# Fillers, paired rstd and moved GpSimd work in the first stage of a spectral and GEGLU layer

## Chip, cores and metric

The kernel runs on one core of a Trainium2 chip. The metric is device time in microseconds (us), the median of several runs. The core has five queues that are spoken of here: PE (TensorE, products; its weight loads are listed as PEld), DVE (VectorE), ACT (ScalarE), POOL (GpSimd) and SP (SyncE, which issues most transfers).

## The reference, cut to what matters

Two sublayers, each with a residual and a layer norm in front, on x of 2048 rows and 576 columns in bf16. The first multiplies the two-dimensional real Fourier transform by a complex weight. The second is a GEGLU feed-forward layer.

```
def _layernorm(x, axis=-1, eps=1e-5):
    m = jnp.mean(x, axis=axis, keepdims=True)
    v = jnp.var(x, axis=axis, keepdims=True)
    return (x - m) / jnp.sqrt(v + eps)
...
X = rfft2(layernorm(x));  y = irfft2(X * (w_r + 1j * w_i))
h = x + y
h2 = h + (gelu(n @ w_gate) * (n @ w_up)) @ w_down      # n = layernorm(h)
```

## The kernel before, in words

The order on every queue is the order of the program text: the author writes it out by hand, and each engine works through its own instructions in that order, waiting on semaphores that the framework derives from the data.

**First stage** (lines 73 to 450, the one that is changed). x is held as 16 tiles h of 128 rows by 576 columns (`h_sb[:, h, :]`), loaded in six chunks (L72: tiles 0-1, 2-3, 4-5, 6-7, 8-11, 12-15). Each tile goes through these steps:

- Statistics into `mv`: on DVE by `ln_dve` (L115 to 119, called through `sd`) for tiles 0, 2, 4, 6, 8, 10 and 12 to 15; on ACT by `ln_act` (L121) for 1, 3, 5, 7, 9 and 11, which `ln_fin` on POOL turns into a variance (L128, L129).
- `ln_rstd` on POOL (L133, L134): adds eps and takes the power -0.5 for a range of tiles.
- `norms(lo, hi)` (L337): per tile a normalisation on DVE into `xn` (L137), then `row16(h)` on PE.
- `row16` (L288): first `fill`, which is a number of filler products of the identity with a slice of x into the PSUM tile that the real products overwrite afterwards; then four products of 256 columns with the table F16 (L298), a Fourier transform over 16 rows; then `row16_rest` (L311), two small products for the remaining columns, which for tiles 12 to 15 come later.
- Evictions from PSUM into `Bt` on ACT (`evict`, L322, for two tiles; `evict4`, L328, for the remaining columns of four tiles, the last of these on DVE).

PSUM tiles come from one pool of four, given out in turn (`two`). A filler that writes such a tile waits until its previous user has been evicted.

Between these steps the text places the making of tables. POOL makes index tables by iota, the column angles `kd` (L198, three operations of 290 columns, and L199, a rounding over all 870 columns), clears `DF`, `DI` and the ends of `Zts`, and gathers reversed rows of both weights into `wm` (L364, indirect transfers). DVE makes the row angles (`angle_a`, `angle_b`, `angle_c`, for k in `first` or `rest`) and `phases` and `drop_sign` for the column angles. ACT makes their sines (`sine`, `cosine`, `col_sin`). SP then moves `wm_r` into `WR` (L412), transposes `TF` into `TI` (L262) and copies parts of the column table `DT` into `DF`, `DI` and `DS` (L424).

The stage ends with the products into `pt` (L435), their scaled copies `G16` on ACT (L443), and three fillers into the second half of the same PSUM tile.

**Behind it:** f2 (L479) multiplies Bt by the column tables, f3 (L494, L495) combines halves, DVE multiplies by the weights (`wmul`), i3 and `inv_cols` (L570 to L619) go back, and `add_rows` (L742) adds the result to x. Then comes the feed-forward part: gate and up products (L877) and down products (L897), in four chunks of 512 rows.

Of the kernel before, what the change touches and what calls it, by code (L numbers as in the profile page):

```python
# [10 lines left out]
ALU = mybir.AluOpType  # L11
# [12 lines left out]
D = 576  # L24
# [17 lines left out]
def kernel_body(  # L42
# [14 lines left out]
    G = nc.gpsimd  # L57
    T = nc.tensor
# [7 lines left out]
    def two(name):  # L66
        return psum.tile([P, 2, 512], FP32, name=name, tag="two", bufs=4)

    h_sb = keep.tile([P, H, D], BF16, name="h_sb")
# [28 lines left out]
    ident = keep.tile([P, P], BF16, name="ident")  # L98
# [7 lines left out]
    DF = keep.tile([P, 2, 2, JH], BF16, name="DF")  # L106
    DI = keep.tile([P, 2, 2, JH], BF16, name="DI")
    DS = keep.tile([P, 2, 2, JH], BF16, name="DS")
    mv = keep.tile([P, H, 2], FP32, name="mv")
    rstd = keep.tile([P, H], FP32, name="rstd")  # L110
# [4 lines left out]
    def ln_dve(dst, h):  # L115
        st = roll.tile([P, 2, 6], FP32, name="st", tag="st", bufs=3)
        V.bn_stats(st[:, 0, :], h_sb[:, h, 0:DH])  # L117
        V.bn_stats(st[:, 1, :], h_sb[:, h, DH:D])  # L118
        V.bn_aggr(dst[:, h, :], st[:])  # L119

    def ln_act(h):  # L121
        for i, fn, sc in ((0, ACT.Identity, 1.0 / D), (1, ACT.Square, 1.0 / D**0.5)):
            junk = roll.tile([P, D], BF16, name="junk", tag="junk", bufs=2)
            A.activation(junk[:], h_sb[:, h, :], fn, scale=sc, accum_out=mv[:, h, i : i + 1])

    def ln_fin(hs):
        sq = roll.tile([P, H], FP32, name="sq", tag="sq", bufs=2)
        G.tensor_tensor(sq[:, hs], mv[:, hs, 0], mv[:, hs, 0], ALU.mult)  # L128
        G.tensor_tensor(mv[:, hs, 1], mv[:, hs, 1], sq[:, hs], ALU.subtract)  # L129

    def ln_rstd(dst, src, lo, hi):
        sl = slice(lo, hi)
        G.tensor_scalar(dst[:, sl], src[:, sl, 1], 1e-5, None, op0=ALU.add)  # L133
        G.tensor_tensor(dst[:, sl], dst[:, sl], mhalf[:, sl], ALU.pow)  # L134
# [33 lines left out]
    def tmp(name, shape, dtype=I32):  # L168
        return scr.tile(shape, dtype, name=name)

    def iota(t, pattern, base=0, cm=0):
        G.iota(t, pattern=pattern, base=base, channel_multiplier=cm, allow_small_or_imprecise_dtypes=True)
# [18 lines left out]
    iJ = tmp("iJ", [P, JP], FP32)  # L191
    iota(iJ[:], [[1, 2], [2, JH]])
    iDs = tmp("iDs", [P, 3], FP32)
    G.tensor_scalar(iDs[:], iD[:], 1.0 / D, None, op0=ALU.mult)
    pd, kd = tmp("pd", [P, 3, JP], FP32), tmp("kd", [P, 3, JP], FP32)
    C23 = 8388608.0
    for t in range(3):
        G.tensor_scalar(kd[:, t, :], iJ[:], iDs[:, t : t + 1], C23, op0=ALU.mult, op1=ALU.add)  # L198
    G.tensor_scalar(kd[:], kd[:], -C23, -float(D), op0=ALU.add, op1=ALU.mult)  # L199
    rev = tmp("rev", [P, 1])  # L200
    iota(rev[:], [[0, 1]], 2 * P - 1, -2)

# [19 lines left out]
    def drop_sign(dst, src):  # L222
        V.tensor_scalar(
            dst.bitcast(I32),
            src.bitcast(I32),
            1,
            1,
            op0=ALU.logical_shift_left,
            op1=ALU.logical_shift_right,
        )  # L230
# [3 lines left out]
    def angle_a(sl):  # L234
        n = sl.stop - sl.start
        V.scalar_tensor_tensor(
            pr[:, sl],
            q16[:].unsqueeze(1).to_broadcast([P, n, P]),
            s2p[:, 0:1],
            ks[:, sl].unsqueeze(2).to_broadcast([P, n, P]),  # L240
            op0=ALU.mult,
            op1=ALU.add,
        )

    def angle_b(sl):
        V.tensor_scalar(pr[:, sl], pr[:, sl], 2047, None, op0=ALU.bitwise_and)
        V.tensor_scalar(ab[:, sl], pr[:, sl], -1024.0, None, op0=ALU.add)

    def angle_c(sl):
        drop_sign(ab[:, sl], ab[:, sl])  # L250

    def sine(sl):
        A.activation(TF[:, sl, 2, :], pr[:, sl], ACT.Sin, bias=pib[:], scale=-2.0 * PI / S)

    def cosine(sl):
        A.activation(TF[:, sl, 1, :], ab[:, sl], ACT.Sin, bias=nhpib[:], scale=2.0 * PI / S)
# [15 lines left out]
    def row_table():  # L272
        V.tensor_tensor(
            F16[:, 0:2, :],
            fs[:].unsqueeze(1).to_broadcast([P, 2, P]),
            mask[:].unsqueeze(1).to_broadcast([P, 2, P]),
            ALU.mult,
        )
        V.tensor_scalar(F16[:, 2, :], F16[:, 0, :], -1.0, None, op0=ALU.mult)
# [3 lines left out]
    def fill(dst, n):  # L283

        for _ in range(n):
            T.matmul(dst, lhsT=ident[:], rhs=h_sb[:, 2, 0:512], start=True, stop=True)  # L286

    def row16(h):  # L288
        if h % 2 == 0 or h == H - 1:
            ps_f[h] = two("f2t")  # L290
        if h % 4 == 0:
            ps_f["f4", h] = two("f4")
        f2t, b = (ps_f[h], 0) if h in ps_f else (ps_f[h - 1], 1)
        fill(f2t[:, b, :], 10 if h == 0 else 1 if h < 12 else 0)
        x = xn[:, h, :]
        for t in range(2):
            for n, d0 in ((0, t * P), (1, DH + t * P)):
                T.matmul(  # L298
                    f2t[:, b, t * 2 * P : (t + 1) * 2 * P],
                    lhsT=x[:, d0 : d0 + P],  # L300
                    rhs=F16[:, n : n + 2, :],
                    start=(n == 0),
                    stop=(n == 1),
                )
        if h < 12:
            row16_rest(h)

    def row16_rest(h):
        o = (h % 4) * P
        for p0, d0 in ((0, 256), (64, 512)):  # L310
            T.matmul(  # L311
                ps_f["f4", h - h % 4][p0 : p0 + 64, 0, o : o + P],
                lhsT=xn[:, h, d0 : d0 + 64],
                rhs=F16[:, 0, :],
                start=True,
                stop=True,
            )

    def evict(*hs):
        for h in hs:  # L320
            n = 1 if h >= H - 2 else 2
            A.copy(  # L322
                Bt[:, 0:4, :].rearrange("p t (c h l) -> p (t c) h l", c=16, h=16)[:, :, h : h + n, :],
                ps_f[h][:, 0:n].rearrange("p h (tc l) -> p tc h l", l=8),
            )

    def evict4(h):
        (V.tensor_copy if h == 12 else A.copy)(  # L328
            Bt[:, 4, :].rearrange("p (c h l) -> p h c l", c=16, h=16)[:, h : h + 4, :, :],
            ps_f["f4", h][:, 0].rearrange("p (h c l) -> p h c l", h=4, c=16),  # L330
        )

    def sd(*hs):
        for h in hs:
            ln_dve(mv, h)

    def norms(lo, hi):  # L337
        for h in range(lo, hi):
            normalise(V, xn[:, h, :], mv, rstd, h)
            row16(h)  # L340
# [14 lines left out]
    first, rest = slice(0, 2), slice(2, 9)  # L355
    ln_act(1)
    ln_act(3)
    sd(0)
    row_table()
    sd(2)  # L360
    ln_fin(slice(1, 4, 2))
    ln_rstd(rstd, mv, 0, 4)
    for t, w in zip(wm, (A_w_r, A_w_i)):
        G.indirect_dma_start(  # L364
            out=t[:],
# [1 line left out]
            in_=w.rearrange("(a r) j -> a (r j)", r=8),  # L367
            in_offset=bass.IndirectOffsetOnAxis(ap=rev[:, 0:1], axis=0),
        )
    sd(4)  # L370
    ln_act(5)
    ln_act(7)
    norms(0, 4)
    evict(0, 2)
    evict4(0)
    sd(6)
    ln_fin(slice(5, 8, 2))
    ln_rstd(rstd, mv, 4, 8)
    G.memset(DF[:], 0.0)
    G.memset(DI[:], 0.0)  # L380
    for z in Zts:
        G.memset(z[:, :, J:], 0.0)
    angle_a(first)
    angle_b(first)
    angle_c(first)
    sine(first)
    cosine(first)
    norms(4, 8)
    ln_act(9)
    ln_act(11)  # L390
    phases()
    drop_sign(kd[:], pd[:])
    sd(8)
# [5 lines left out]
    evict4(4)  # L399
    col_sin(1, pd, zerob)  # L400
    col_sin(0, kd, hpib)
    sd(12)
    norms(8, 12)
    sd(13)
    ln_rstd(rstd, mv, 12, 14)
    sd(14, 15)
    ln_rstd(rstd, mv, 14, 16)
    evict(8, 10)
# [21 lines left out]
    evict4(12)  # L430
    angle_b(rest)
    pt = two("pt")
    for x in range(2):
        for p0 in (0, 64):
            T.matmul(  # L435
                pt[p0 : p0 + 64, 0, x * P : (x + 1) * P],
                lhsT=F16[:, 0, 64 * x : 64 * x + 64],
                rhs=ident[:],
                start=True,
                stop=True,  # L440
            )
    for sign in range(2):
# [4 lines left out]
            scale=G_SCALE if sign == 0 else -G_SCALE,  # L447
        )
    sine(rest)
    fill(pt[:, 1, :], 3)  # L450

    def weights():
        V.tensor_scalar(WI[:, 9 : H + 1, 0:J], wm[1][:].rearrange("p (r j) -> p r j", r=8), -1.0, None, op0=ALU.mult)
# [397 lines left out]
    for h in range(4, H):  # L851
        b = 6 * (h // 2 - 2)
# [4 lines left out]
        b = h // 4 * NFT - NFT + 3 * (h % 4) + 2 + 12 * (h < 8)  # L857
# [6 lines left out]
    for tcnk in range(4):  # L864
        for gi in range(NG):
# [5 lines left out]
            for i in range(FQ):  # L871

                gu = two("gu")
                for r in range(NR):
                    for c in range(2):
# [3 lines left out]
                            lhsT=w[rows, r, i * P : (i + 1) * P],  # L879
                            rhs=hl[tcnk % 2][rows, r, :],  # L880
                            start=(r == 0),
                            stop=(r == NR - 1),
# [7 lines left out]
        for st in range(4):  # L890
            h = tcnk * 4 + st
            last = h == H - 1
            acc = two("acc")
            for c in range(2):
                cc = slice(c * DH, (c + 1) * DH)
                for f in range(NFT):
                    T.matmul(  # L897
                        acc[:, c, 0:DH],
                        lhsT=p_sb(f)[:, st * P : (st + 1) * P],
                        rhs=wd[f // NWA][:, f % NWA, cc],  # L900
                        start=(f == 0),
                        stop=(f == NFT - 1),
# [60 lines left out]
```

## Time and profile before

| What | Value |
|---|---|
| Median of three runs | 510.25 us (509.28 to 511.15) |
| The profiled execution's own time | 510.21 us |
| Its span, first to last instruction | 508.3 us |
| PE busy | 493.3 us, 97% of the span |
| DVE, ACT, POOL busy | 212.7, 151.6, 28.4 us |
| First product of f2 (L479) | 31.73 us |
| First gate product (L877) | 79.37 us |

An entry of a timeline gives start, duration, engine, line, operation, the result and its sources, and how many there were in a row; brackets hold the idle time of the engine before it and what ended it. Matmuls overlap, so their durations are longer than their spacing. The table of stretches gives busy time of PE, PEld, DVE, ACT and POOL with the number of instructions, then the clock granted to PE (1.00 is full), the share of the transfer engines and GB/s. "issue" in the chain of work is time in which the engine waited for nothing that the profile shows.

### The profile page before, as it was taken

To read this page: it belongs to the slowest core of one execution; us is meant where nothing else is said; L and a number is where in the kernel's file an instruction comes from. 1 tells how busy PE (TensorE), PEld (TensorE's weight loads), DVE (VectorE), ACT (ScalarE), POOL (GpSimd) and SP (SyncE) were. 2 spreads that over 40 slices of the span, in tenths; PEclk is the share of its full clock that TensorE was granted. 3 is DMA by queue.
4 is the path that set the end of the run, shared out by engine and by line. 5 is a ranking of instruction groups with operands and counts; after the bars stand their busy time and mean duration, and the time that the engine had idled before them with its cause. 6 is when DMAs were issued, how large, how long until landed. Compare 5 with 4: busy or idle time off the path is not lost.

```text
span 508.3 us, 9886 instructions
## 1 busy us (share of the span) xinstructions
PE 493.3 (97%) x4334; PEld 291.7 (57%) x4334; DVE 212.7 (42%) x421; ACT 151.6 (30%) x265; POOL 28.4 (6%) x75
## 2 busy tenths in 40 slices
PE   6799999999999999999999999999999999999996
PEld 2367775555558774444468744444578544444775
DVE  7879974689662015433311034433201233333001
ACT  6879984232220002323210023233200133332000
POOL 8300010111110000000000000000000000000000
PEclk9899999999999999999999999999999999999999
DMA  9408957779970009998730089987500488870000
GB/s 295 157 19 160 242 156 208 150 150 188 189 155 0 1 36 195 201 190 151 148 62 1 1 181 196 190 165 153 98 0 1 120 167 158 157 148 1 12 14 25
DMA packets 88200, 61.54 MB, mean 121 GB/s; under 512 B 22813, under 2 KB 86749, under 8 KB 88157
## 3 DMA queue, kind: packets, MB, share of 16 engines
q1 hardware_dynamic: 87869, 59.72, 59.0%
q0 software_dynamic: 288, 1.18, 0.6%
q8 instruction: 34, 0.56, 0.5%
q14 instruction: 9, 0.07, 0.1%
HBM read 52.65 MB, written 2.36 MB: 108 GB/s over the span
## 4 chain that ended last, share of the span: by engine, by line
PE 91%; DVE 3%; POOL 2%; ACT 1%; issue 1%; DMA 1%; POOLq 0%
PE gu L877 55%; PE acc L897 28%; PE pq_ps L479 2%; PE cs_ps L619 1%; PE eo_ps L572 1%; PE y_ps L742 1%; PE eo_ps L570 1%; DMA Bt<-hrow 1%; PE gh_ps L495 1%; POOL rstd L134 1%; DVE xn L137 1%; ACT Bt L322 1%; DVE h_sb L787 1%; PE f2t L298 1%; PE gh_ps L494 1%
## 5 line engine op out<-in xcount | busy, mean ns | idle before, releaser
L877 PE MATMUL gu<-Bt,wgu 64*128 64x512 bf16 x2592 | 281.5, 376 | 1.0 <-DMA Bt<-hrow 1.0
L877 PEld LDWEIGHTS <-wgu 64*128 64x128 bf16 x2592 | 131.2, 94 | 148.1 <-issue 2.0
L885 ACT ACTIVATE g_sb<-gu 128x512 f32<-128x512 f32 x144 | 86.1, 598 | 302.8 <-PE gu L877 302.8
L886 DVE TENSOR_TENSOR P_sb<-g_sb,gu 128x512 bf16<-128x512 f32 x144 | 98.8, 686 | 153.0 <-ACT g_sb L885 153.0
L897 PEld LDWEIGHTS <-P_sb 128*128 128x128 bf16 x1152 | 112.4, 98 | 30.6 <-issue 2.4
L897 PE MATMUL acc<-wd,P_sb 128*128 128x288 bf16 x768 | 99.3, 286 | 0.0
L909 DVE TENSOR_TENSOR h_sb<-h_sb,acc 128x576 bf16<-128x576 bf16 x15 | 11.3, 755 | 118.2 <-PE acc L897 118.2
L897 PE MATMUL acc<-wd_a,P_sb 128*128 128x288 bf16 x384 | 52.3, 286 | 0.5 <-DVE h_sb L905 0.5
L298 PE MATMUL f2t<-F,xn 128*128 128x256 bf16 x64 | 11.5, 320 | 3.7 <-DVE xn L137 3.7
L286 PE MATMUL f2t<-h_sb,ident 128*128 128x512 bf16 x21 | 9.6, 547 | 4.3 <-DMA h_sb<-in_A_x_dram 4.3
L479 PE MATMUL pq_ps<-DT,Bt 128*128 128x290 bf16 x64 | 12.2, 286 | 0.0
L767 DVE TENSOR_SCALAR hrow<-h_sb,mv,rstd 128x1152 bf16<-128x1152 bf16 x14 | 12.1, 867 | 0.0
L134 POOL TENSOR_TENSOR rstd<-rstd,mhalf 128x1 f32<-128x1 f32 (+2 forms) x17 | 11.4, 673 | 1.4
L298 PEld LDWEIGHTS <-xn 128*128 128x128 bf16 x64 | 6.8, 111 | 8.1 <-DVE xn L137 5.4
L619 PEld LDWEIGHTS <-EO 128*128 128x128 bf16 x96 | 9.1, 96 | 3.0 <-issue 0.2
L479 PEld LDWEIGHTS <-Bt 128*128 128x128 bf16 x96 | 9.3, 97 | 2.5
L487 ACT CAST pq<-pq_ps 128x580 bf16<-128x580 f32 x15 | 9.8, 662 | 1.7 <-PE pq_ps L479 1.6
L133 POOL TENSOR_SCALAR rstd<-mv 128x1 f32<-128x1 f32 (+2 forms) x17 | 4.0, 235 | 112.6 <-DVE mv L119 112.4
L322 ACT CAST Bt<-f2t 128x1024 bf16<-128x1024 f32 (+1 forms) x9 | 8.1, 926 | 6.9 <-PE f2t L298 6.9
L117 DVE BATCH_NORM_STATS2 st<-h_sb 128x6 f32<-128x288 bf16 x22 | 9.8, 444 | 0.0
L118 DVE BATCH_NORM_STATS2 st<-h_sb 128x6 f32<-128x288 bf16 x22 | 9.7, 442 | 0.0
L619 PE MATMUL cs_ps<-DI,EO 128*128 128x290 bf16 x32 | 9.1, 285 | 0.0
(130 smaller groups left out, 252.3 us busy)
## 6 DMA issues: line engine op xcount, KB each, us to landing
wgu<-in_B_w_gate_dram SPq DMA_DIRECT2D x48, 432.0 KB, 5.1
wgu<-in_B_w_up_dram SPq DMA_DIRECT2D x48, 432.0 KB, 6.5
wd<-in_B_w_down_dram SPq DMA_DIRECT2D x2, 1728.0 KB, 7.5
wd_a<-in_B_w_down_dram SPq DMA_DIRECT2D x1, 1728.0 KB, 14.6
out_dram<-h_sb SPq DMA_DIRECT2D x3, 576.0 KB, 3.5
h_sb<-in_A_x_dram SPq DMA_DIRECT2D x4, 288.0 KB, 3.3
h_sb<-in_A_x_dram SPq DMA_DIRECT2D x2, 576.0 KB, 5.2
WR<-in_A_w_r_dram SPq DMA_DIRECT2D x1, 650.2 KB
```

The source lines that it names most:

```text
L117: V.bn_stats(st[:, 0, :], h_sb[:, h, 0:DH])
L134: G.tensor_tensor(dst[:, sl], dst[:, sl], mhalf[:, sl], ALU.pow)
L298: T.matmul(f2t[:, b, t * 2 * P : (t + 1) * 2 * P], lhsT=x[:, d0 : d0 + P], rhs=F16[:, n : n + 2, :], start=(n == 0), stop=(n == 1),)
L322: A.copy(Bt[:, 0:4, :].rearrange("p t (c h l) -> p (t c) h l", c=16, h=16)[:, :, h : h + n, :], ps_f[h][:, 0:n].rearrange("p h (tc l) -> p ...
L479: T.matmul(ps[:, par, 0:JP], lhsT=Bt[:, t, col], rhs=DT[:, t // 2, par] if t < 4 else DF[:, par], start=(t == par), stop=(t == 4),)
L619: T.matmul(ps[:, e, 0:JP], lhsT=EO[x][:, 2 * e + jt if jt < 2 else 4, 2 * g : 2 * g + 2].rearrange("p h e k l -> p (h e k l)"), rhs=DI[:, ...
L767: V.tensor_scalar(hrow[:], h_sb[:, h, :].rearrange("p (r k) -> p r k", k=64).unsqueeze(2).to_broadcast([P, NR, 2, 64]), mv2[:, h, 0:1], rs ...
L877: T.matmul(gu[:, c, :], lhsT=w[rows, r, i * P : (i + 1) * P], rhs=hl[tcnk % 2][rows, r, :], start=(r == 0), stop=(r == NR - 1),)
L885: A.activation(g_sb[:], gu[:, 0, :], ACT.Gelu_apprx_tanh)
L886: V.tensor_tensor(p_sb(fa + i), g_sb[:], gu[:, 1, :], ALU.mult)
L897: T.matmul(acc[:, c, 0:DH], lhsT=p_sb(f)[:, st * P : (st + 1) * P], rhs=wd[f // NWA][:, f % NWA, cc], start=(f == 0), stop=(f == NFT - 1),)
L909: V.tensor_tensor(hv, hv, acc[:, :, 0:DH], ALU.add)
```

## The change

The functions stay; what changes is the number of fillers, one operand, and the order of the text. Fillers read x tile 0 rather than tile 2. Their numbers are 8 before tile 0 (10 before the change), 3 before tile 2, 5 before tile 4, 16 before tile 8, 4 before tile 12, none before 13 to 15, and one before every other tile; the three at the end of the stage become four and are placed ahead of the products into pt. In all there are 48 fillers rather than 24. The first four values of rstd come in two pairs, and tiles 0 and 1 are normalised after the first. The memsets of DF and DI move into the setup; the operations on kd move behind the first values of rstd; the gathers and the memsets of Zts move behind the rounding of kd. On DVE, the statistics of tiles 4 and 6 stand between the two pairs, and those of tile 13 ahead of the normalisation of tiles 8 to 11.

```
     iDs = tmp("iDs", [P, 3], FP32)
+    G.memset(DF[:], 0.0)
+    G.memset(DI[:], 0.0)
     G.tensor_scalar(iDs[:], iD[:], 1.0 / D, None, op0=ALU.mult)
     pd, kd = tmp("pd", [P, 3, JP], FP32), tmp("kd", [P, 3, JP], FP32)
     C23 = 8388608.0
-    for t in range(3):
-        G.tensor_scalar(kd[:, t, :], iJ[:], iDs[:, t : t + 1], C23, op0=ALU.mult, op1=ALU.add)
-    G.tensor_scalar(kd[:], kd[:], -C23, -float(D), op0=ALU.add, op1=ALU.mult)
...
-            T.matmul(dst, lhsT=ident[:], rhs=h_sb[:, 2, 0:512], start=True, stop=True)
+            T.matmul(dst, lhsT=ident[:], rhs=h_sb[:, 0, 0:512], start=True, stop=True)
...
-        fill(f2t[:, b, :], 10 if h == 0 else 1 if h < 12 else 0)
+        fill(f2t[:, b, :], {0: 8, 2: 3, 4: 5, 8: 16, 12: 4, 13: 0, 14: 0, 15: 0}.get(h, 1))
...
     ln_act(1)
     ln_act(3)
     sd(0)
+    ln_fin(slice(1, 2))
+    ln_rstd(rstd, mv, 0, 2)
     row_table()
     sd(2)
-    ln_fin(slice(1, 4, 2))
-    ln_rstd(rstd, mv, 0, 4)
+    ln_fin(slice(3, 4))
+    ln_rstd(rstd, mv, 2, 4)
+    norms(0, 2)
+    ln_act(5)
+    ln_act(7)
+    ln_act(9)
+    for t in range(3):
+        G.tensor_scalar(kd[:, t, :], iJ[:], iDs[:, t : t + 1], C23, op0=ALU.mult, op1=ALU.add)
+    sd(4, 6)
+    norms(2, 4)
+    evict(0, 2)
+    evict4(0)
+    ln_fin(slice(5, 8, 2))
+    ln_rstd(rstd, mv, 4, 8)
+    G.tensor_scalar(kd[:], kd[:], -C23, -float(D), op0=ALU.add, op1=ALU.mult)
+    angle_a(first)
+    angle_b(first)
+    angle_c(first)
+    sine(first)
+    cosine(first)
+    norms(4, 8)
+    ln_act(11)
     for t, w in zip(wm, (A_w_r, A_w_i)):
         G.indirect_dma_start(
...
-    sd(4)
-    ln_act(5)
-    ln_act(7)
-    norms(0, 4)
-    evict(0, 2)
-    evict4(0)
-    sd(6)
-    ln_fin(slice(5, 8, 2))
-    ln_rstd(rstd, mv, 4, 8)
-    G.memset(DF[:], 0.0)
-    G.memset(DI[:], 0.0)
     for z in Zts:
         G.memset(z[:, :, J:], 0.0)
-    angle_a(first)
-    angle_b(first)
-    angle_c(first)
-    sine(first)
-    cosine(first)
-    norms(4, 8)
-    ln_act(9)
-    ln_act(11)
     phases()
...
-    sd(12)
+    sd(12, 13)
+    ln_rstd(rstd, mv, 12, 14)
     norms(8, 12)
-    sd(13)
-    ln_rstd(rstd, mv, 12, 14)
     sd(14, 15)
...
     pt = two("pt")
+    fill(pt[:, 1, :], 4)
     for x in range(2):
...
     sine(rest)
-    fill(pt[:, 1, :], 3)
```

## The prediction

> **What bounds the kernel now.** All times are microseconds (us) in one profiled execution. I first read the page's chain of work that ended last: 91% of the span is TensorE (PE). The stages behind the first one run densely, so what counts is when the first stage hands over, which is the first product of L479. The same chain in order of time ends that stage so:
>
> ```profile
> 28.57 1.90 ACT Bt L322 x3
> 30.47 0.57 ACT G L443 x2
> 31.09 0.81 PE pt L286 x3
> 31.89 2.24 PE pq_ps L479 x18
> ```
> The reader should see the last evictions of Bt, then the two G16 copies, then three fillers that wait for these copies, and only then the real products. The timeline of PE puts the first of these products at 31.73.
>
> Next the timeline of PE in the first stage (start, duration, instruction, in brackets the idle time before it):
>
> ```profile
> 11.27 0.39 PE L286 MATMUL f2t<-h_sb,ident 128*128 128x512 bf16 x1
> 11.49 0.60 PE L298 MATMUL f2t<-F,xn 128*128 128x256 bf16 x4
> ...
> 15.32 0.61 PE L298 MATMUL f2t<-F,xn 128*128 128x256 bf16 x4 [1.79 <-DVE xn L137]
> ...
> 18.90 1.06 PE L298 MATMUL f2t<-F,xn 128*128 128x256 bf16 x4
> ...
> 22.28 0.61 PE L298 MATMUL f2t<-F,xn 128*128 128x256 bf16 x4 [1.57 <-DVE xn L137]
> ```
> The same four products take 0.60 or 1.06. The stretches of one us, whose third last column is the granted clock, say why:
>
> ```profile
> 16.00:17.00 1.00, 1.00 (x10) 0.55 (x9) 1.00 (x3) 1.00 (x4) 0.00 (x0) 1.00 0.35 108
> 18.00:19.00 1.00, 1.00 (x6) 0.36 (x5) 0.97 (x4) 0.92 (x2) 0.20 (x1) 0.50 0.60 183
> 22.00:23.00 1.00, 0.72 (x6) 0.42 (x7) 1.00 (x4) 1.00 (x2) 0.00 (x0) 1.00 0.00 0
> 25.00:26.00 1.00, 1.00 (x6) 0.28 (x5) 0.97 (x5) 0.00 (x0) 0.34 (x1) 0.50 0.17 40
> ```
> Twice the clock is halved for about 3.4 us (17.1 to 20.5 and 24.0 to 27.4, from the partial shares beside these rows), and each time PE had waited for xn in the 3.4 us ahead. Such a stretch costs 1.7 us of PE work.
>
> Why PE waits is in the timeline of VectorE (DVE) and, beside it, that of GpSimd (POOL):
>
> ```profile
> 13.65 1.61 DVE L137 TENSOR_SCALAR xn<-h_sb,mv,rstd 128x576 bf16<-128x576 bf16 x1 [1.27 <-POOL rstd L134]
> 21.80 1.45 DVE L137 TENSOR_SCALAR xn<-h_sb,mv,rstd 128x576 bf16<-128x576 bf16 x4 [0.63 <-POOL rstd L134]
> ...
> 13.57 0.57 POOL L379 MEMSET DF<- 128x580 bf16 x1
> 14.10 0.57 POOL L380 MEMSET DI<- 128x580 bf16 x1
> 14.62 0.48 POOL L382 MEMSET Zt<- 128x124 bf16 x3
> ```
> One normalisation lasts 1.61, where four in a row elsewhere last 1.45, 0.36 each. It lies beside POOL's memsets and ends 0.16 after them (15.10 against 15.26). So POOL's back-to-back operations hold up this form of DVE operation, and DVE, busy otherwise, is what PE waits for.
>
> **The change, step by step.** I walk each queue forward with durations of these rows.
>
> Start. The fillers now read x tile 0. ScalarE's first read of that chunk starts at 3.48, tile 2 was there at 4.33. Eight fillers at 0.44 (ten took 4.42) run from 3.5 to 7.0.
>
> POOL loses the kd products and rounding here (3.89 to 6.31) and gains the memsets of DF and DI (0.52 each by the starts above), done at about 4.5; iDs and rev follow, until 5.0. No row shows these memsets beside DVE's small operations at 3.33 to 3.9 (ks, iu, mask): they cost between 0, if they slip between, and 1.05, if held to the end. I take 1.05, as the nearest row is the normalisation above. The statistics of tile 0 then run 4.9 to 5.85.
>
> Rstd in pairs. A product and a power for two columns took 24.31 to 25.34, so rstd(0,2) is ready at 6.95. DVE meanwhile makes F16 (0.7) and the statistics of tile 2 (0.97), to 7.5, and the normalisations of tiles 0 and 1 end at 8.2. Before, they began at 8.63. PE waits from 7.0 to 7.9. The statistics of tiles 4 and 6 follow, to 10.15. POOL has rstd(2,4) at 8.6, then the kd products (1.7), to 10.3, which hold tiles 2 and 3 for 0.15: done at 11.05, angles (10.96 to 12.38, 1.4) at 12.45.
>
> Tiles 4 to 7. Their four POOL operations took 2.14 (11.47 to 13.61): 10.3 to 12.45. The kd rounding now stands right behind, 0.63 to its follower, 0.92 in duration. It holds DVE for between 0 and 0.92; I take 0.92, since POOL goes on without a wait. Tiles 4 to 7 run 13.4 to 14.85, where they ended at 16.27. The memsets of Zt come behind both gathers and meet only phases and drop_sign, at most 0.48.
>
> Tiles 8 to 15. Phases, drop_sign, the statistics of 8 and 10 and minus_sine take 3.96 (16.20 to 20.16): to 18.8. Statistics of 12 and 13 take 1.95: 20.75. Rstd(8,12) took 1.6 behind tile 10's statistics, ready at 20.3: its wait of 0.63 is covered by tile 13. Tiles 8 to 11 are normalised at 22.2, statistics 14 and 15 end at 24.1, tiles 12 and 13 at 24.8. Rstd(14,16) took 1.2 behind the statistics (26.07 to 27.27): 25.3. Tiles 14 and 15 run 25.3 to 26.0; before, from 27.31 on. DVE gains 2.0.
>
> PE. One tile takes 0.93 with its filler at full clock (10.56 to 11.49), 0.70 without, 1.64 halved. From 7.9 with the clock low until about 10.3 as now: tile 0 to 9.2, one filler, tile 1 to about 10.8, three fillers, tiles 2 and 3 to 13.05, five fillers to 14.1; xn(4) is there at 13.8. Tiles 4 to 7 take 3.5: 17.6. Sixteen fillers at 0.215 (three at 31.09 to 31.73) take 3.4: 21.0, and xn(8) comes at 21.15. Tiles 8 to 11 take 3.5, four fillers 0.85: 25.5. Tiles 12 to 15 take 0.53 each: 27.6 (xn(14) at 25.7 is no wait). Their rests take 0.41 (29.12 to 29.53), four fillers now **ahead** of the pt products 0.86, these 0.30: PE is free at **29.2**. The last evictions (0.92, 0.5, 0.5 behind tile 13 at 26.6) end at 28.5, so Bt is not late.
>
> Handover. L479 starts at 29.2, not 31.73: **2.5 us earlier**. Then ScalarE copies G16 (to 29.85), makes the sine (1.09) and starts the first pq copy at 30.9, while its reader f3 has its place on PE at 31.6. That is no wait. SyncE and the gathers: wm_r is asked for at 13.4, not 8.80. If it takes the same 6.4, SP goes on at 20.0 (now 15.23); WR, the transpose and DF take 0.74, 1.32 and 1.27, landing 2.7 later: 26.1, cover 3.1 us. A gather later by more than that delays the handover one for one. wm_i is read at 32 and has more cover.
>
> Twenty-four fillers more (48 against 24) cost 5.2 us of PE at full clock; they stand in waits, apart from the four ahead of tile 12, 0.85 on PE's path. If the waits were gone, all would be on it.
>
> [...]
>
> **Sum.** The profiled execution took 510.21 (span 508.3 and 1.91 around it). Less 2.5: 507.7. Its time stands 0.04 under the median of 510.25, so I forecast the median with it. Best bound: DVE is held nowhere, minus 1.05 early and 0.92 later, of which PE's queue lets through some 0.6: 507.1. Worst bound of the unknowns alone: PE starts warm one 3.4 us window later, 1.7 of PE work, of which 0.9 shows because of the idle time at xn(4) and xn(8): 508.6.
>
> **Rivals.**
> 1. One half-clock stretch stays, because the wait at 7.0 to 7.9, or one that I missed, starts it. For it: waits of 1.6 were enough twice. Against: a wait of 1.24 at 29.84 was not followed by one. PE has no slack behind 17.6, so 1.7 of the 2.5 goes: 509.4.
> 2. Slower: the fillers do not hold the clock, whatever they fill. PE's queue from 13.8 to 29.2 is full, so each half-clock stretch adds 1.7. It decides from 2.5 / 1.7 = 1.5 stretches on: with two, 510.21 - 2.5 + 3.4 = 511.1; with three, 512.8. For it: sixteen fillers at 0.40 (25.58 to 25.98) would be 6.4 rather than 3.4. [...]
> 3. The change does not do what it says: fillers wait for their PSUM tile (as the three at 31.09 do now), or DVE is held longer, and only the earlier handover at pt is won. ScalarE's evictions then still end at 30.4, pt is no longer waited for, and 31.73 becomes 30.5: 509.0.
>
> **Chances.** Forecast 0.76, rival 1 with 0.10, rival 2 with 0.08 (half of it at 512.8), rival 3 with 0.06. About 0.3%, 1.5 us, is what a measurement of this kernel can tell from no change: faster means under 508.7. That is the forecast alone, 0.76; within 0.3% are rivals 1 and 3 and half of 2, 0.20; slower 0.04. The range goes from 506.8 (the best bound, with 0.3 for the spread of runs of 509.28 to 511.15) to 509.4, which takes in rivals 1 and 3.
>
> **What would show it.** Right: granted clock 1.0 from 11 us on; no PE wait above 1 us behind 8; xn(8) near 20.8; no normalisation of 1.6; first L479 product near 29.2; L877 begins 2.5 before 79.37. Wrong: a normalisation held beside POOL's kd operations by more than 0.9; sixteen fillers that take over 4 us or end well behind xn(8); DF landing behind 29; an L479 start that moves without L877 moving.

## The result and the profile after

The changed kernel takes **507.49 us** (median of four runs, 507.37 to 508.24) against 510.25 us (509.28 to 511.15): 2.76 us less. The ratio, which goes by all runs rather than by the medians, is 0.9949, 95% interval 0.9929 to 0.9970. Measured again later it was 507.40 us over six runs, ratio 0.9955 (0.9937 to 0.9973). The times of the kernel before lie near 509.15, 510.2 or 511.2 us, for a reason that is not shown, so its median shifts (in the later measurement it is 509.15, and the medians differ by only 1.75) and the ratios are the better measure.

The profiled execution took 508.24, the slowest of the four. Its clock row on the page (40 slices) no longer has the 8 that the page of before has in its second slice, the one from 12.7 to 25.4:

```profile
PEclk9999999999999999999999999999999999999999
```

Here is the timeline of PE in the first stage, with the fillers (L285), the products of a tile (L297) and the first products of f2 (L480, which was L479):

```profile
11.79 1.06 PE L297 MATMUL f2t<-F,xn 128*128 128x256 bf16 x4
...
13.18 0.60 PE L297 MATMUL f2t<-F,xn 128*128 128x256 bf16 x4
...
18.50 3.63 PE L285 MATMUL f2t<-h_sb,ident 128*128 128x512 bf16 x16
21.96 0.60 PE L297 MATMUL f2t<-F,xn 128*128 128x256 bf16 x4
...
29.74 0.67 PE L480 MATMUL pq_ps<-DT,Bt 128*128 128x290 bf16 x4
```
Once tile 2 is through, four products always last 0.60, and no wait of PE behind 8 us is longer than 0.2. The handover to f2 is at 29.74; it was at 31.73. In this execution the clock, by the durations, rose only after the products of tile 2 (1.06). In the profiled execution of the later measurement it rose ahead of tile 0, and the same kernel hands over another 0.7 earlier:

```profile
7.68 0.61 PE L297 MATMUL f2t<-F,xn 128*128 128x256 bf16 x4 [0.71 <-DVE xn L137]
...
13.87 0.61 PE L297 MATMUL f2t<-F,xn 128*128 128x256 bf16 x4 [0.75 <-DVE xn L137]
...
21.22 0.61 PE L297 MATMUL f2t<-F,xn 128*128 128x256 bf16 x4 [0.20 <-DVE xn L137]
...
29.01 0.67 PE L480 MATMUL pq_ps<-DT,Bt 128*128 128x290 bf16 x4
```

Next come DVE and POOL in the first of these two executions. The holds that the prediction priced can be read one by one:

```profile
3.32 1.23 DVE L216 TENSOR_SCALAR ks<-kv,s2p 128x9 f32<-128x9 f32 x1
3.46 1.15 DVE L217 TENSOR_SCALAR iu<-iu 128x128 int32<-128x128 int32 x1
...
12.67 2.19 DVE L137 TENSOR_SCALAR xn<-h_sb,mv,rstd 128x576 bf16<-128x576 bf16 x4 [0.60 <-POOL rstd L134]
...
25.31 0.77 DVE L137 TENSOR_SCALAR xn<-h_sb,mv,rstd 128x576 bf16<-128x576 bf16 x2 [0.60 <-POOL rstd L134]
```

```profile
3.41 0.59 POOL L194 MEMSET DF<- 128x580 bf16 x1
3.93 0.59 POOL L195 MEMSET DI<- 128x580 bf16 x1
...
12.73 0.93 POOL L376 TENSOR_SCALAR kd<-kd 128x870 f32<-128x870 f32 x1
```
A DVE operation on nine columns lasts 1.23 (0.23 before) because POOL's two memsets lie beside it; an experiment below takes them away, and it is 0.23 again. The four normalisations from 12.67 last 2.19 rather than 1.45: POOL's rounding of kd starts 0.06 behind the first of them and ends at 13.66 (12.73 + 0.93). Tiles 14 and 15 are normalised from 25.31; it was 27.31.

All of the gain is made by the handover. The time of a profiled execution less the start of its first f2 product is 510.21 - 31.73 = 478.48 before, 508.24 - 29.74 = 478.50 after, and 507.50 - 29.01 = 478.49 in the second execution. In all runs below it lies between 478.3 and 478.6. So nothing behind the first stage gained or lost, and the start of the first f2 product can be used as the measure.

### The profile page after: what moved, and what is told of

Its sections match the earlier page's. It is cut to its first block, busy times and chain, and to the rows that moved or that the text cites. A ratio compares the mean times of both kernels' runs of the same rounds, so it can differ in the third digit from the quotient of the medians.

```text
span 506.3 us, 9938 instructions
## 1 busy us (share of the span) xinstructions
PE 496.3 (98%) x4356; PEld 292.9 (58%) x4358; DVE 213.0 (42%) x421; ACT 151.5 (30%) x265; POOL 30.0 (6%) x79
## 4 chain that ended last, share of the span: by engine, by line
PE 92%; DVE 4%; POOL 1%; DMA 1%; issue 1%; ACT 0%; POOLq 0%; DVEq 0%
PE gu L878 55%; PE acc L898 28%; PE pq_ps L480 2%; PE cs_ps L620 1%; PE f2t L285 1%; PE eo_ps L573 1%; PE y_ps L743 1%; PE f2t L297 1%; PE eo_ps L571 1%; DMA Bt<-hrow 1%; PE gh_ps L496 1%; DVE h_sb L788 1%; PE gh_ps L495 1%; DVE xn L137 0%; POOL rstd L134 0%
## 5 line engine op out<-in xcount | busy, mean ns | idle before, releaser
L898 PEld LDWEIGHTS <-P_sb 128*128 128x128 bf16 x1152 | 112.4, 98 | 30.6 <-issue 2.4
L285 PE MATMUL f2t<-h_sb,ident 128*128 128x512 bf16 x42 | 13.8, 451 | 3.7 <-DMA h_sb<-in_A_x_dram 3.7
L480 PE MATMUL pq_ps<-DT,Bt 128*128 128x290 bf16 x64 | 12.3, 286 | 0.0
L297 PE MATMUL f2t<-F,xn 128*128 128x256 bf16 x64 | 10.5, 300 | 0.6 <-DVE xn L137 0.4
L480 PEld LDWEIGHTS <-Bt 128*128 128x128 bf16 x96 | 9.2, 97 | 2.3
L285 PEld LDWEIGHTS <-ident 128*128 128x128 bf16 x48 | 4.7, 106 | 9.0 <-issue 2.8
L297 PEld LDWEIGHTS <-xn 128*128 128x128 bf16 x64 | 6.7, 106 | 4.5 <-DVE xn L137 1.3
```

Of the source, the lines that this page charges most:

```text
L285: T.matmul(dst, lhsT=ident[:], rhs=h_sb[:, 0, 0:512], start=True, stop=True)
L297: T.matmul(f2t[:, b, t * 2 * P : (t + 1) * 2 * P], lhsT=x[:, d0 : d0 + P], rhs=F16[:, n : n + 2, :], start=(n == 0), stop=(n == 1),)
L480: T.matmul(ps[:, par, 0:JP], lhsT=Bt[:, t, col], rhs=DT[:, t // 2, par] if t < 4 else DF[:, par], start=(t == par), stop=(t == 4),)
L898: T.matmul(acc[:, c, 0:DH], lhsT=p_sb(f)[:, st * P : (st + 1) * P], rhs=wd[f // NWA][:, f % NWA, cc], start=(f == 0), stop=(f == NFT - 1),)
```

## The experiments

All ten ran beside the kernel before; seven are the changed kernel with one or two edits, one repeats it, and two combine one half of the change with the other half of before. The later places of the kd operations and of the gathers were not undone alone.

**The order without the fillers.** The changed order of the text, with the fillers, their places and their operand (x tile 2) as before:

```
-        fill(..., {0: 8, 2: 3, 4: 5, 8: 16, 12: 4, 13: 0, 14: 0, 15: 0}.get(h, 1))
+        fill(f2t[:, b, :], 10 if h == 0 else 1 if h < 12 else 0)
...
-    fill(pt[:, 1, :], 4)      # ahead of the pt products
+    fill(pt[:, 1, :], 3)      # behind sine(rest)
```


> The changed order of the text with the fillers of before (10, then 1 per tile up to 11, three behind G16). Theory (order and fillers both count): tiles 4 to 7 are worked through at about 17.2, xn(8) comes near 21.2, PE idles some 4 us, the clock halves behind that, and the three end fillers wait for G16: L479 starts near 30.5, total 508.9 (508.4 to 509.6), with a granted clock of 0.5 somewhere in 20 to 26. Rival (the order on VectorE does it all): clock stays, L479 near 29.4, total 507.7 or less.

Measured: 509.92, against 510.17 for the kernel before, run beside it, ratio 0.9998 (0.9989 to 1.0006). No difference can be seen. The handover of the profiled execution is at 31.76, as before the change. Here are PE's timeline and the stretches (third last column the clock):

```profile
21.22 1.04 PE L297 MATMUL f2t<-F,xn 128*128 128x256 bf16 x4 [3.44 <-DVE xn L137]
...
24.48 1.06 PE L297 MATMUL f2t<-F,xn 128*128 128x256 bf16 x4
```

```profile
20.00:21.00 1.00, 0.00 (x0) 0.00 (x0) 0.97 (x4) 0.66 (x1) 0.62 (x2) 0.50 1.03 305
24.00:25.00 1.00, 1.00 (x6) 0.52 (x5) 0.71 (x3) 0.95 (x1) 0.75 (x2) 0.50 0.20 37
27.00:28.00 1.00, 1.00 (x11) 0.85 (x11) 0.15 (x1) 0.90 (x1) 0.00 (x0) 1.00 0.32 71
```
xn(8) is as early as in the changed kernel, and DVE's last two normalisations start as early (25.32). PE gives all of it back: it waits 3.44, the clock is halved from 20.0 to about 26.8, twice as long as any stretch of before, and the tiles behind take 1.64 each. I expected one such stretch and 508.9 (508.4 to 509.6); in this execution it was two, and the median lies above that range. The rival that the order on DVE does it all falls.

**The fillers without the order.** The text of before with the 48 fillers, which read x tile 0.

> The order of before with the changed fillers (48 of them, four ahead of the pt products). Theory: no half-clock stretch behind 13 us; xn(8) still at 22.2, sixteen fillers end at about 22.6, then PE's own queue leads to L479 at about 30.6: total 509.1. [...]

Measured: 508.91 against 510.17, ratio 0.9989 (0.9978 to 1.0000), and the handover at 30.56 where I expected 30.6:

```profile
15.80 0.60 PE L298 MATMUL f2t<-F,xn 128*128 128x256 bf16 x4
...
22.78 0.60 PE L298 MATMUL f2t<-F,xn 128*128 128x256 bf16 x4
...
30.56 0.67 PE L479 MATMUL pq_ps<-DT,Bt 128*128 128x290 bf16 x4
```
Both half-clock stretches behind 13 us are gone in this execution, though no step of DVE has moved (its normalisations start at 13.63, 21.80 and 27.32, within 0.02 of before). So here the fillers held the clock where they fill the wait: its column is 1.00 in every stretch from 13 to 34 us, and was 0.50 at 18 and at 25 before. Behind tile 0 PE then waits for nothing: the sixteen fillers end 0.6 behind xn(8), and the queue of PE sets the handover.

One wait is left, of 1.99 ahead of tile 0, which in the changed kernel the pairs of rstd shorten. In six of the twelve runs the mean granted clock is 0.995 to 0.997, and one stretch of 3.4 us at half clock makes 0.9966 of a span of 507 us. So about one stretch seems to remain in these six. Where it lies is not shown, as none of the six has a trace; the experiment without pairs has one behind just this wait. In all ten runs of the changed kernel the mean is 0.999 or 1.000.

**The end fillers back behind G16.**

```
-    fill(pt[:, 1, :], 4)      # ahead of the pt products
+    fill(pt[:, 1, :], 3)      # behind sine(rest)
```


> The changed kernel, but with the three end fillers behind G16 again rather than four ahead of pt. Theory: PE waits for the last eviction and for G16, then for three fillers: L479 near 30.7 rather than 29.74, total 508.4. Rival (the end fillers cost their own time in either place): one filler fewer, 507.3.

Measured: 508.38 (ratio to before 0.9971, 0.9960 to 0.9981), 0.98 more than the 507.40 of the changed kernel. The wait of before is back, with the same 1.24:

```profile
29.30 0.81 PE L285 MATMUL pt<-h_sb,ident 128*128 128x512 bf16 x3 [1.24 <-ACT G L444]
29.95 0.66 PE L480 MATMUL pq_ps<-DT,Bt 128*128 128x290 bf16 x4
```
The handover is 0.94 later than the 29.01 of the early execution; I had counted the expected 30.7 from the late one (29.74). Behind G16 these fillers cost one us. Ahead of pt they cost some 0.3 by an estimate: in the early execution of the changed kernel the last evictions into Bt, which f2 reads, end at 28.68, and f2 starts at 29.01. No run leaves the end fillers out.

```profile
26.69 1.99 ACT L321 CAST Bt<-f2t 128x1024 bf16<-128x1024 f32 x3 [0.52 <-PE f2t L297]
```

**No fillers ahead of tile 8.** In the table of fillers `8: 16` becomes `8: 0`.

> The changed kernel without the sixteen fillers ahead of tile 8. Theory (half a window of waiting halves the clock): PE idles from about 18.4 to 21.2, tile 8 starts 0.8 earlier, but a stretch of 0.5 of some 3.4 us follows and costs 1.7, less what of it falls into the wait: L479 near 30.4, total 508.2. [...]

Measured: 508.90 (507.40 to 510.16; ratio 0.9981, 0.9970 to 0.9992), handover at 30.48.

```profile
21.22 0.61 PE L297 MATMUL f2t<-F,xn 128*128 128x256 bf16 x4 [3.76 <-DVE xn L137]
...
23.71 1.06 PE L297 MATMUL f2t<-F,xn 128*128 128x256 bf16 x4
...
30.48 0.67 PE L480 MATMUL pq_ps<-DT,Bt 128*128 128x290 bf16 x4
```
The clock is 0.50 from 22.3 to 25.7, as the theory has it, and the handover is where the theory put it (30.4). The theory's half window was an estimate from the 1.57 and 1.79 of idle time ahead of the two stretches of 3.4 in the kernel before; a wait of 3.76 does not show how short one can be. The expected total was still 0.7 too low: 30.4 and the 478.5 behind the handover make 508.9, but I had added to the median of 507.49 from the handover of 29.74, which belongs to the execution of 508.24.

The mean granted clock of the twelve runs prices a stretch. The one run of 507.40 has 0.999, no stretch; nine of 508.79 to 509.05 have 0.995 to 0.997, about one; two of 510.04 and 510.16 have 0.993, about two. So the first costs 1.5 here and the second 1.2. In the one run without a stretch the kernel is as fast as with the sixteen fillers, so what they are worth is the clock.

**Rstd of the first four tiles at once.** The pairs are undone; everything else stays as changed.

```
-    ln_fin(slice(1, 2))
-    ln_rstd(rstd, mv, 0, 2)
     row_table()
     sd(2)
-    ln_fin(slice(3, 4))
-    ln_rstd(rstd, mv, 2, 4)
+    ln_fin(slice(1, 4, 2))
+    ln_rstd(rstd, mv, 0, 4)
```


> The changed kernel with the first four values of rstd made at once, behind the statistics of tiles 0 to 3. Theory (the pairs matter through PE's clock, not through VectorE): tiles 0 and 1 are normalised 1.4 later, but tile 4 is held by the kd rounding until 13.3 anyway, so VectorE's times from tile 4 on stay within 0.2; PE waits some 1.9 between the first fillers and tile 0, so the clock rises a window later: total 507.5 to 508.3. Rival (VectorE's start decides): the 1.4 comes through, 508.8.

Measured: 509.14 (508.43 to 510.54; ratio to before 0.9990, 0.9977 to 1.0002), 1.7 more than the changed kernel. My expectation was too low, and the rival's 508.8 nearer. PE and DVE:

```profile
9.39 0.61 PE L297 MATMUL f2t<-F,xn 128*128 128x256 bf16 x4 [2.15 <-DVE xn L137]
...
12.59 1.06 PE L297 MATMUL f2t<-F,xn 128*128 128x256 bf16 x4
...
22.89 0.60 PE L297 MATMUL f2t<-F,xn 128*128 128x256 bf16 x4
```

```profile
8.90 0.90 DVE L137 TENSOR_SCALAR xn<-h_sb,mv,rstd 128x576 bf16<-128x576 bf16 x2 [1.56 <-POOL rstd L134]
...
14.32 1.49 DVE L137 TENSOR_SCALAR xn<-h_sb,mv,rstd 128x576 bf16<-128x576 bf16 x4
```
Both theories hold a part. DVE starts tile 0 1.65 later and ends tile 7 at 15.81 rather than 14.86, 0.95 later: the kd rounding (13.32 to 14.24) now runs beside the angles and holds no normalisation, so the hold that I meant to cover the delay is gone, but only 0.7 of the 1.65 is regained. PE waits 2.15 ahead of tile 0; the clock falls to 0.50 from about 10.6 to 14.0, and tile 8 starts at 22.89 rather than 21.22 (21.96 in the late execution of the changed kernel). How much of the 1.7 is the clock's and how much DVE's is not separated.

**Tile 13's statistics back behind the normalisations of tiles 8 to 11.**

> The changed kernel with tile 13's statistics back behind the normalisations of tiles 8 to 11. Theory: xn(14) comes about 0.75 later, near 26.5, which PE with its four fillers ahead of tile 12 reaches at about the same time: at most 0.2, total 507.4 to 507.7. Rival (VectorE's end decides, as my step by step sum has it): 508.1.

Measured: 507.49 (ratio 0.9950, 0.9935 to 0.9965). Tiles 14 and 15 are normalised from 26.11, 0.8 later, and the handover is at 29.12, 0.1 later than the early one. With four fillers ahead of tile 12, PE does not need xn(14) sooner, so this move of DVE's work was worth nothing in this kernel.

**Fewer fillers, and memsets out of DVE's way.** Four kernels run side by side: the changed kernel again, it with `8: 12` and `12: 0`, it with the memsets of DF and DI behind `ln_fin(slice(9, 12, 2))`, and both edits.

> The changed kernel once more, on the chip of the runs beside it: 507.5, with single runs near 507.4 where the clock rises before the first tiles are through and near 508.2 where it rises one window later.

> The changed kernel with twelve fillers ahead of tile 8 instead of sixteen and none ahead of tile 12 instead of four. Theory (from tile 8 on PE's own queue, fillers in it, sets the handover): the four ahead of tile 12 come off in full, 0.86, until xn(14) at 25.7 is waited for: L479 0.85 earlier, total 506.6. Rival (VectorE sets it): no change, 507.4. Rival (the fillers ahead of tile 12 hold the clock): a stretch of 0.5 behind 25, 508 or more.

> The changed kernel with the memsets of DF and DI taken out of the setup and put behind the variance of tiles 9 and 11. Theory: ks and iu on VectorE last 0.23 again rather than 1.23 and 1.15, tile 0's statistics start 0.9 earlier, of which ScalarE's statistics and POOL's kd work let 0.45 through to tile 4 and to the handover: 507.0. Rival (the whole hold reaches the handover): 506.5. Rival (it is hidden): 507.4.

> The two edits before this together: fewer fillers, and the memsets of DF and DI late. Theory: with PE's queue shorter, VectorE sets the handover and what it gains at tile 4 comes through: 506.2. Rival (PE's queue still sets it): as with fewer fillers alone, 506.6.

| Kernel | Median us | Ratio to before (95%) | First f2 product |
|---|---|---|---|
| changed, again | 507.40 | 0.9955 (0.9937 to 0.9973) | 29.01 |
| fewer fillers | 506.75 | 0.9942 (0.9924 to 0.9960) | 28.33 |
| DF, DI late | 507.10 | 0.9949 (0.9931 to 0.9967) | 28.78 |
| both | **506.37** | 0.9935 (0.9916 to 0.9953) | 27.92 |

The kernel before, run beside them, has a median of 509.15 us. Runs of one changed kernel differ here by 0.4 at most, so the differences of 0.65, 0.30 and 1.03 stand clear. The three edited kernels lie 0.1 to 0.2 above what the theories said; with both edits 506.37 lies between the theory (506.2) and its rival (506.6).

Most of the cost of fillers that stand in no wait is paid: four ahead of tile 12 fill 0.87 (24.75 to 25.62), and without them the products of tiles 12 to 15 take 2.10 rather than 1.91, so 0.68 is left at the handover. The twelve fillers ahead of tile 8 do something that I had not looked for. In the profiled execution with fewer fillers the clock rose as late as in the slowest one of the changed kernel (tile 2's products take 1.06), yet tile 8 starts at 21.22, as in the early one. The shorter row takes up the late rise, which costs 0.7 with sixteen.

The memsets delay the statistics of tile 0 by 0.93 (4.79 against 3.86). Without them tile 0 is normalised only 0.50 earlier, as DVE then waits 0.35 for rstd (POOL, by my estimate, for ScalarE's statistics); tile 8 is 0.24 earlier, and the handover 0.23 in the traces, 0.30 in the medians. Here are the two edits in the timelines, DVE's ks with the memsets late, and PE with both edits:

```profile
3.32 0.23 DVE L214 TENSOR_SCALAR ks<-kv,s2p 128x9 f32<-128x9 f32 x1
```

```profile
16.77 2.77 PE L283 MATMUL f2t<-h_sb,ident 128*128 128x512 bf16 x12
20.81 0.61 PE L295 MATMUL f2t<-F,xn 128*128 128x256 bf16 x4 [1.27 <-DVE xn L137]
...
27.92 0.67 PE L480 MATMUL pq_ps<-DT,Bt 128*128 128x290 bf16 x4
```
The wait of 1.27 that the shorter row of fillers leaves is not followed by a lower clock in this trace, and the mean clock is 1.00 in all six runs. This version beats both kernels: it is 1.03 below the changed one and takes 0.9935 of the time before.

## Why the prediction was right, point by point

- **Handover and sum.** Forecast: L479 2.5 earlier, at 29.2, and 507.7. Measured: 2.0 earlier in one trace (29.74), 2.7 in the other (29.01); 507.49. The forecast lies between because it let the clock rise at 10.3: in the traces it rose at about 12.7 and ahead of 7.7. That it lies between them is luck. The late one is the worst bound of the prediction (508.6, with 0.9 for the late rise; that it comes 3.4 later was an estimate from the length of a stretch); it took 508.24, and the late rise cost 0.7. Of the ten runs of this kernel it is the only one above 507.6. The time of 507.7 is 29.2 plus the 478.5 behind the handover; the gain of 2.5 hangs on which execution of before it is counted from.
- **DVE.** The ends of the steps in its queue met the trace within 0.4, and within 0.25 from tile 7 on. The price of the early memsets, for which I took the upper bound of 1.05, came to 0.93. That tile 7 ends at 14.86, forecast 14.85, has two errors in it that cancel: the kd rounding held the four normalisations by 0.74 (2.19 against 1.45) rather than 0.92, and their rstd came 0.2 late. Two slips in the working carry no term of the sum: the rounding's row before the change ends at 6.60, not 6.31, and its follower starts 0.88 behind it, not 0.63. The sign "xn(8) near 20.8" is the start of that normalisation (20.79); the working itself has xn(8) at 21.15.
- **PE.** Tile 4 at 14.1: 14.98 and 13.87. Tile 8 at 21.15: 21.96 and 21.22. The sixteen fillers took 3.46, forecast 3.4. The tiles follow the moment of the first rise of the clock, until the late xn(8) evens part of it out. The sign of a clock of 1.0 from 11 us on holds in the clock's column, but not by the durations of the late execution, which are those of a low clock until 12.7.
- **SyncE and the gathers.** I had wm_r take 6.4 and SP go on at 20.0; it went on at 18.41, as the transfer took 4.6. But the transpose then took 2.19 rather than 1.32, and the copies into DF 1.69 rather than 1.27, and they landed 3.9 rather than 2.7 after their issue. DF was there at about 26.2, forecast 26.1, so the cover was what I said, by errors that cancel.
- **Rival 1** (one half-clock stretch stays, 509.4) did not come: no run of the changed kernel shows a stretch in its mean clock. The wait ahead of tile 0 was 0.71 where the clock was already up, and 0.44 where it was not yet. The experiments without pairs and without the sixteen fillers show such a stretch: with one the handover is at 30.67 (DVE's delay included) and 30.48.
- **Rival 2** (the clock halves whatever is filled, 511.1) is refuted by the trace with the fillers alone and by the changed kernel: behind 13 us the clock's column is 1.00 in both. The five traced falls stand behind waits of 1.57 and 1.79 (before), 2.15 (no pairs) and 3.76 (no fillers ahead of tile 8), and some 2.2 into the wait of 3.44 (order alone).
- **Rival 3** (only the handover at pt is won, 1.2): that part is worth 0.98.
- **What the forecast did not see** is how the parts depend on each other. By the ratios, order alone is worth nothing that can be seen (0.9998), the fillers alone with their new place at the end 0.1%, some 0.6 us (0.9989, interval to 1.0000), and both together 0.45% to 0.51%, 2.3 to 2.6 us. Order makes xn earlier, which only lengthens PE's wait at tile 8 and brings on the low clock; fillers hold the clock but lengthen PE's queue. I summed both on one path without pricing either alone. The pairs had no term of their own and are worth 1.7. What the two stretches cost the kernel before is open: five of its 61 runs beside the experiments have a mean clock of 1.00, no stretch, and take 509.10 to 509.23, only some 1.0 below the profiled execution, but the mean does not show when the clock first rose.
- I counted the four fillers ahead of tile 12 as 0.85 on PE's path; taking them off (with four ahead of tile 8) gave 0.65, as xn(14) is waited for next. I named tile 13's move as what covers rstd(8,12); undone, it costs 0.1, as PE is late there.

## What to carry to other kernels

Where PE waits in short pieces, look at the granted clock behind the wait before counting the wait itself: here a halved clock behind a wait cost 1.5 us in a kernel whose wait itself cost nothing. Fill such waits, and size the row of fillers to end a little ahead of the data; most of what goes beyond that is on the path (0.68 of 0.87 ahead of tile 12), and a row that is a little short (a wait of 1.27 here) kept the clock and took up a late start of it. Put GpSimd's longer operations beside statistics (0.41 and 0.44 beside the kd products here, as elsewhere), not beside the normalisations that others wait for (0.92 rather than 0.72), and take each half of such a change alone, for neither may be worth much without the other.

## What the runs showed of the hardware that was not expected

- The clock was halved behind or within waits of 1.57 to 3.76 us. It was not behind waits of 1.24 (end of the stage, before the change) and 1.27 (both edits). Behind the 1.99 of the fillers alone the clock's column is 1.00, but the durations are those of a low clock on both sides of it (eight fillers 3.57, a tile's products 1.04). In the trace of the kernel before the clock rises at 10.3 (by the durations), falls at 17.1 and 24.0 and rises at 20.5 and 27.4: whole multiples of about 3.4 apart. In the 3.4 us just ahead of each of the five falls PE was idle for 1.57 to 2.4. Why a wait of 1.27 and one of 1.57 differ, no run shows.
- A stretch lasted about 3.4 us where PE was full from its start, and about 6.8 in the one trace where PE was idle for its first 1.2 (order without fillers, 20.0 to 26.8).
- When the clock first rises differs between executions of one kernel (ahead of 7.7 or at 12.7 us in two traces), and with it the handover by 0.7. Why is not shown. The clock column of the stretches shows 1.00 there though eight fillers took 3.57 and a tile's products 1.06; that it was low there is read from the durations alone.
- Statistics on DVE (0.41 and 0.44, as elsewhere) did not lengthen beside POOL's kd products, whereas two normalisations beside them took 0.92 rather than 0.72.
